# Two weight DMAs on two queues, 33 warm-up matmuls and two clamps on VectorE in a linear-attention and gated-MLP block

## The chip, the cores and the metric

The kernel runs on one core of a Trainium2 chip. A core has TensorE (PE, matmuls; its weight loads are listed as PEld), VectorE (DVE), ScalarE (ACT), GpSimd (POOL) and SyncE (SP), which here only issues DMAs. The engines run side by side, each through its own instructions in order, and wait for each other by semaphores. The metric is the device time of one execution in microseconds; lower is better.

## The reference

The input x has 2048 tokens of 448 features. The block is linear attention with 16 heads of 28 features, behind a LayerNorm, and a gated MLP with 1792 hidden features, behind another one; both add to their input. All tensors are bfloat16.

```python
def _A_ref(x, wqkv, wo):
    q, k, v = split(x @ wqkv)                       # 16 heads of 28
    phi = lambda t: jnp.where(t > 0, t + 1, jnp.exp(t)) + 1e-6
    pq, pk = phi(q), phi(k)
    kv = jnp.einsum("bhsd,bhse->bhde", pk, v)
    z = jnp.einsum("bhsd->bhd", pk)
    num = jnp.einsum("bhqd,bhde->bhqe", pq, kv)
    den = jnp.einsum("bhqd,bhd->bhq", pq, z)[..., None] + 1e-6
    return merge(num / den) @ wo

def _B_ref(x, w_gate, w_up, w_down):
    return (_gelu(x @ w_gate) * (x @ w_up)) @ w_down

h = x + _A_ref(_layernorm(x), A_wqkv, A_wo)
h2 = h + _B_ref(_layernorm(h), B_w_gate, B_w_up, B_w_down)
```

## The kernel before, in words

Tokens are worked in 16 tiles of 128. Every piece of work is a named task on one engine, and the tasks' order on each engine is written out in full in `ORDERS` (line 14), one string for each of PE, ACT, DVE, POOL and SP. A task that needs another engine's result waits for that engine's counter; a DMA has a semaphore of its own. An engine does not look past a task that waits. A number behind a name is the tile (k14 is the K and V matmuls of tile 14) or, for gu, the group.

1. *Start.* PE runs `warm1` and `warm0` (line 457: `WARM` matmuls of 128 columns on ones), which need no input. Meanwhile the x tiles are loaded. For each tile `bnst`, `bnag` (VectorE) make mean and variance, `ln`, `rstd` (ScalarE) the factor, and `norm` the normalised tile: on VectorE for tiles 0 to 3, on GpSimd for the others, with the negated mean from `negm`.
2. *Transposes.* Tiles 0 to 3 are transposed on PE (`tr`, line 495) and copied out of PSUM by ScalarE (`ev`). Tiles 4 to 15 get 64 of their columns copied by ScalarE (`dup`) and are transposed by a DMA on SyncE (`xT`).
3. *K and V, queries.* `k` and `v` of a tile (lines 561 and 562) are 14 matmuls that use the two row halves of PE at once, on two PSUM banks that they fill crosswise. ScalarE makes the exponential (`ek`) and copies V (`evv`), `cl` clamps the exponential (line 566), `ph` on VectorE adds max(K, eps) to the clamped value, and `acc..a`, `acc..b` add K-transposed times V into banks 6 and 7. The two `acc` halves of a tile use the banks crosswise, and so wait for each other when they are neighbours of different kind. Query chunks (`qa`, `qb`) stand between, with `eq` (ScalarE), `cq` (clamp, GpSimd) and `pq` (sum, VectorE); for later chunks `rq` on ScalarE and `cq`, `pq` on VectorE.
4. *Hand-over.* `kz1`, `kz2` mask the sums, `nd` multiplies with the queries, `rd` and `om` divide, `tro`/`evo` or the DMA `oT` transpose, `wo` is the output projection, `hr` the residual add, and the second LayerNorm follows with `hbnst`, `hbnag`, `hln`, `hrstd`, `normh`. `wrap` copies a few columns so that the transposed halves are complete; for tiles 0 and 1 PE transposes (`trh`, line 702) and `evh` copies out.
5. *MLP.* The 56 groups `gu` (line 811) make gate and up on the two row halves, `ge` is the Gelu on ScalarE (after the table load `tbl2`), `hm` the product on VectorE, `down` the last projection, `out` the residual and `dout` the store. The remaining `nd`, `wo` and LayerNorm work is spread between the groups.

The gate and up weights lie in one tile, `wgu_sb`: gate in partitions 0 to 63, up in 64 to 127, seven slices of 64 rows each. They come by fourteen DMAs, gate and up by turns, all on SyncE, after the last `xT` and the four loads of `wo`:

```python
for k in range(7):
    prev = [dma(wgu_sb[0:64, k, :], wg3[:, k, :], [b_wg[k]], "dwg%d" % k, 64 * FF * 2, after=prev, key=20.0)]
    prev = [dma(wgu_sb[64:128, k, :], wu3[:, k, :], [b_wu[k]], "dwu%d" % k, 64 * FF * 2, after=prev, key=20.0)]
```

The down weights (`dwd`) follow behind oT2 and oT3.

## Time and profile before

| | |
|---|---|
| median of 3 runs | 196.68 us (196.2 to 196.69) |
| the profiled execution | 196.7 us, of which its span is 194.9 |
| PE busy | 190.3 us, 98% of the span |
| DVE, ACT, POOL busy | 116.3, 78.2, 42.0 us |
| PE matmuls of gate and up | 980, 90.4 us busy |
| PE matmuls of down (row halves / whole array) | 336, 34.4 us / 70, 10.8 us |
| DMA | 17.53 MB, 90 GB/s over the span |

In the rows below, a timeline line is the start, the length of the stretch, engine, source line, operation, output and inputs, and the count of instructions merged; square brackets give the engine's idle time before it and what ended it. A line of a group gives busy time, the mean of one in ns, and the idle time before. A row of stages gives the stretch, its length, the busy us of PE, PEld, DVE, ACT and POOL with their instructions, the granted clock, the share of DMA time and GB/s. Line 430 is the helper of nearly all paired matmuls, so these are told apart by their tiles.

### The profile page before, as it was taken

The numbers are of one execution on the slowest core, as the hardware profiler recorded it, in microseconds if no ns is written. First come the engines' busy times: TensorE is split into PE (matmuls) and PEld (weight loads), VectorE is DVE, ScalarE is ACT, GpSimd is POOL, SyncE is SP. The second block draws the span as 40 slices with busy tenths as digits, with TensorE's granted clock in tenths as the row PEclk, the third lists the DMA queues.
The fourth block names the chain that finished last, engine by engine and source line by source line (L and its number), as shares of the span: only waits on it lengthen the run. The fifth ranks groups of instructions, "written<-read, shape, count | busy, mean of one in ns | idle before, by whom it ended". The sixth has DMA issues, their size and how long they took to land.

```text
span 194.9 us, 5336 instructions
## 1 busy us (share of the span) xinstructions
PE 190.3 (98%) x2192; PEld 137.9 (71%) x2192; DVE 116.3 (60%) x301; ACT 78.2 (40%) x205; POOL 42.0 (22%) x90
## 2 busy tenths in 40 slices
PE   7999999999999999999999999999999999999994
PEld 7556658754588977976675577877778779899554
DVE  2989735368998946843967745756735443431512
ACT  3689866669784212220442441233232442411100
POOL 3099974300050310500500500500500000000000
PEclk9999999999999999999999999999999999999999
DMA  6944558999836052152062250172040000010111
GB/s 191 377 116 97 81 110 185 247 248 205 260 103 110 15 101 50 50 105 62 10 129 46 46 106 2 30 117 51 5 94 28 23 0 0 3 47 3 47 47 47
DMA packets 37256, 17.53 MB, mean 90 GB/s; under 512 B 28272, under 2 KB 36336, under 8 KB 37232
## 3 DMA queue, kind: packets, MB, share of 16 engines
q1 hardware_dynamic: 36352, 16.45, 36.8%
q10 hardware_dynamic: 880, 0.75, 1.2%
q8 instruction: 17, 0.28, 0.6%
q14 instruction: 7, 0.06, 0.1%
HBM read 8.72 MB, written 1.84 MB: 54 GB/s over the span
## 4 chain that ended last, share of the span: by engine, by line
PE 96%; issue 1%; ACT 1%; DVE 1%; POOL 0%; DVEq 0%; ACTq 0%; POOLq 0%
PE ps L430 87%; PE ps L780 6%; PE ps L454 2%; DVE x_sb L660 1%; PE ps L495 1%; ACT xn L617 1%; PE ps L681 0%; ACT xnT L523 0%; PE ps L672 0%; DVE x_sb L756 0%; POOL ones_bf L395 0%; POOL eps_t L398 0%; ACT pqT L616 0%; DVEq L196 0%; ACTq L196 0%
## 5 line engine op out<-in xcount | busy, mean ns | idle before, releaser
L430 PE MATMUL ps<-hnT,wgu_sb 64*128 64x512 bf16 (+1 forms) x980 | 90.4, 333 | 0.0
L430 PEld LDWEIGHTS ps<-hnT,wgu_sb 64*128 64x128 bf16 x980 | 64.5, 94 | 18.6 <-DVE hh L832 1.7
L830 ACT ACTIVATE gl<-ps 128x256 bf16<-128x256 f32 x112 | 36.9, 381 | 89.3 <-PE ps L430 88.2
L832 DVE TENSOR_TENSOR hh<-ps,gl 128x256 bf16<-128x256 f32 x112 | 42.5, 415 | 35.7 <-ACT gl L830 31.5
L430 PE MATMUL ps<-wd_sb,hh 64*128 64x448 bf16 x336 | 34.4, 349 | 0.0
L430 PEld LDWEIGHTS ps<-wd_sb,hh 64*128 64x128 bf16 x336 | 25.6, 94 | 6.2 <-DVE x_sb L756 0.2
L430 PE MATMUL ps<-wkv_sb,xnT 64*128 64x448 bf16 x192 | 22.4, 350 | 0.4 <-ACT xnT L523 0.4
L462 DVE BATCH_NORM_STATS2 st<-x_sb 128x6 f32<-128x448 bf16 x32 | 18.7, 611 | 2.6 <-DMA x_sb<-in_A_x_dram 2.6
L756 DVE TENSOR_TENSOR x_sb<-ps,x_sb 128x448 bf16<-128x448 f32 (+1 forms) x17 | 9.9, 591 | 16.6 <-PE ps L430 9.8
L474 POOL TENSOR_SCALAR ln<-mv 128x2 f32<-128x2 f32 x7 | 1.6, 223 | 75.0 <-DVE mv L463 74.9
L568 DVE SCALAR_TENSOR_TENSOR pk<-ps,tm 128x448 bf16<-128x448 f32 x16 | 9.8, 620 | 9.6 <-POOL tm L566 7.1
L430 PE MATMUL ps<-xnT,wq_sb 64*128 64x512 bf16 x112 | 14.9, 377 | 0.2 <-ACT xn L617 0.2
L430 PEld LDWEIGHTS ps<-wkv_sb,xnT 64*128 64x128 bf16 x192 | 10.1, 94 | 6.3 <-issue 0.8
L430 PE MATMUL ps<-wo_sb,oT 64*128 64x448 bf16 x98 | 12.1, 350 | 0.1
L660 DVE TENSOR_TENSOR x_sb<-ps,x_sb 128x448 bf16<-128x448 f32 x16 | 9.4, 618 | 4.6 <-PE ps L430 4.4
L780 PE MATMUL ps<-wd_sb,hh 128*128 128x448 bf16 (+1 forms) x70 | 10.8, 315 | 0.0
L566 POOL TENSOR_SCALAR tm<-e 128x448 bf16<-128x448 bf16 x16 | 8.9, 559 | 6.4 <-ACT e L565 5.5
L487 POOL TENSOR_SCALAR hn<-x_sb,nm,rs 128x448 bf16<-128x448 bf16 x14 | 10.0, 720 | 0.8 <-POOL rs L476 0.2
L565 ACT ACTIVATE e<-ps 128x448 bf16<-128x448 f32 x16 | 8.5, 541 | 3.5 <-PE ps L430 2.2
L780 PEld LDWEIGHTS ps<-wd_sb,hh 128*128 128x128 bf16 x70 | 6.7, 98 | 4.3 <-issue 0.4
L655 DVE TENSOR_TENSOR o_sb<-ps,rd 128x448 bf16<-128x448 f32 x16 | 9.4, 612 | 0.1
L570 ACT ACTIVATE v<-ps 128x448 bf16<-128x448 f32 x16 | 8.4, 542 | 2.1 <-PE ps L430 2.1
(69 smaller groups left out, 140.4 us busy)
## 6 DMA issues: line engine op xcount, KB each, us to landing
out_dram<-x_sb SPq DMA_DIRECT2D x15, 112.0 KB, 1.7
wgu_sb<-in_B_w_gate_dram SPq DMA_DIRECT2D x7, 224.0 KB, 6.1
wgu_sb<-in_B_w_up_dram SPq DMA_DIRECT2D x7, 224.0 KB, 6.4
wd_sb<-in_B_w_down_dram SPq DMA_DIRECT2D x1, 1568.0 KB, 8.3
x_sb<-in_A_x_dram SPq DMA_DIRECT2D x2, 448.0 KB, 5.3
wkv_sb<-in_A_wqkv_dram ACTq DMA_DIRECT2D x2, 336.0 KB, 3.7
x_sb<-in_A_x_dram SPq DMA_DIRECT2D x3, 224.0 KB, 4.2
wo_sb<-in_A_wo_dram SPq DMA_DIRECT2D x2, 336.0 KB, 4.4
```

The costliest lines, as they stand in the source:

```text
L430: ins = e.matmul(o_, l_, r_, start=s_, stop=p_, **kw)
L462: op("dve", lambda e: e.bn_stats(st[:, t, :], src_ap), [b_src], [b_st[t]], "%sbnst%d" % ("" if mv is mv1 else "h", t), 0.53, key, after=after)
L487: return lambda e: e.tensor_scalar(dst, src[:, t, :], nm[:, t:t + 1], rs[:, t:t + 1], ALU.add, ALU.mult)
L565: act_exp(lambda e: e.activation(e1[:, ie, :], oK, AF.Exp), bank(bk), [b_e1[ie]], "ek%d" % t, _c_act(D), kk)
L566: op("pool", lambda e: e.tensor_scalar(tm1[:, ie, :], e1[:, ie, :], 1.0 + EPS, 0.0, ALU.min, ALU.max), [b_e1[ie]], [b_tm1[ie]], "cl%d" % t ...
L568: op("dve", lambda e: e.scalar_tensor_tensor(pk[:, i, :, 0:GW], psK3, EPS, tm1[:, ie, :].rearrange("p (g e) -> p g e", g=NG), ALU.max, ALU ...
L655: op("dve", lambda e: e.tensor_tensor(o_sb[:, so, oc:oc + D].rearrange("p (a e) -> p a e", e=28), nd3[:, :, 0:28], rd[:, i, :].unsqueeze(2 ...
L660: op("dve", lambda e: e.tensor_tensor(h_sb[:, u, :], ps[:, b, 0:D], x_sb[:, u, :], ALU.add), bank(b) + [b_x[u]], [b_h[u]], "hr%d" % u, 0.5 ...
L756: op("dve", lambda e: e.tensor_tensor(x_sb[:, t, c0:c1], ps[:, bk, c0:c1], h_sb[:, t, c0:c1], ALU.add), bank(bk) + [b_h[t]], [bo], "out%d% ...
L780: ins = e.matmul(ps[:, bk, c0:c1], hh[:, j, hsl(t)], wd_sb[:, j, c0:c1], start=(j == 0), stop=(j == NJ - 1))
L830: G.add("act", lambda e, gi=gi, cs_=cs_, psG=psG: e.activation(gl[:, gi, cs_], psG[:, cs_], AF.Gelu_apprx_tanh), r=bank(BK_G[i]), w=[b_glh ...
L832: op("dve", lambda e, dst=dst, srcU=srcU, srcL=srcL: e.tensor_tensor(dst, srcU, srcL, ALU.mult), bank(BK_U[i]) + [b_glh], [b_ar[j_][t % HR ...
```

## The change

- The fourteen weight DMAs become two: `dwg`, all of gate, on SyncE behind the `wo` loads, and `dwu`, all of up, on ScalarE's queue. `dwu` waits for the last transposed x tile; it stands between ek13 and ek14 in ScalarE's order.
- `WARM` goes from 38 to 33.
- `cl14` and `cl15` run on VectorE, between ph13 and ph15, instead of GpSimd.
- `trh` waits for the wrapped columns only ahead of its seventh transpose.
- All five orders are written anew. What moves around the steps above: acc3a and acc4a go ahead of and behind q01's second half, acc8b and acc9b behind k11 and k12, acc13a and acc14a ahead of qa20, and acc15a behind qb20; qb31 goes from between wo2a and wo2b to behind trh0; ScalarE runs dup7 and dup6 ahead of ek3, evh0 ahead of eq14, and rq14 later; VectorE runs pkones first, om4 ahead of om5, and cq14 and cq10 behind hm1; GpSimd runs negm12 ahead of cq1, norm13 ahead of norm10, and powwarm at the start. Some gate/up groups near the end change places with the down groups between them.

```diff
-    "... v5 k6 qa01 v6 qb01 k7 acc3a acc4a v7 ..."
+    "... v5 acc3a k6 qa01 v6 qb01 acc4a k7 acc4b acc5b v7 ..."
-    "... k15 acc10a v14 acc10b acc11b v15 acc11a acc12a acc12b acc13b qa20 acc13a acc14a qb20 acc14b acc15b acc15a qa11 ..."
+    "... k14 k15 v14 acc10b acc11b v15 acc11a acc12a acc12b acc13b acc13a acc14a qa20 acc14b acc15b qb20 acc15a qa11 ..."
-    "... qa31 wo2a qb31 wo2b trh1 trh0 nd4a nd4b gu1 gu0 ..."
+    "... qa31 wo2a wo2b trh1 trh0 qb31 nd4a nd4b gu1 gu0 ..."
...
+    CL_DVE = cfg.get("cl_dve", (14, 15))
-    WARM = 38
+    WARM = 33
...
-        for k in range(7):
-            prev = [dma(wgu_sb[0:64, k, :], wg3[:, k, :], [b_wg[k]], "dwg%d" % k, 64 * FF * 2, after=prev, key=20.0)]
-            prev = [dma(wgu_sb[64:128, k, :], wu3[:, k, :], [b_wu[k]], "dwu%d" % k, 64 * FF * 2, after=prev, key=20.0)]
+        prev = [dma(wgu_sb[0:64, :, :], wg3, [*b_wg], "dwg", 7 * 64 * FF * 2, after=prev, key=20.0)]
+        dma(wgu_sb[64:128, :, :], wu3, [*b_wu], "dwu", 7 * 64 * FF * 2, q="act", r=[b_xnT[T - 1]], key=20.0)
...
-            op("pool", lambda e: e.tensor_scalar(tm1[:, ie, :], e1[:, ie, :], 1.0 + EPS, 0.0, ALU.min, ALU.max),
-               [b_e1[ie]], [b_tm1[ie]], "cl%d" % t, 0.53, kk)
+            op("dve" if t in CL_DVE else "pool", lambda e: e.tensor_scalar(tm1[:, ie, :], e1[:, ie, :], 1.0 + EPS, 0.0, ALU.min, ALU.max),
+               [b_e1[ie]], [b_tm1[ie]], "cl%d" % t, _c_dve(D, 4.0) if t in CL_DVE else 0.53, kk)
...
-            def ftrh(e):
+            def ftrh(e, W):
...
-                for k in (0, 1, 2, 4, 5, 6, 3):
+                for n, k in enumerate((0, 1, 2, 4, 5, 6, 3)):
+                    if n in (0, 6):
+                        W(n)
```

## The prediction

> **What bounds the kernel now.** I read the page first, then the busy time by stage, then the chain of work that ended last in order of time, then the timelines of single engines around each edited place.

> ```profile
> span 194.9 us, 5336 instructions
> PE 190.3 (98%) x2192; PEld 137.9 (71%) x2192; DVE 116.3 (60%) x301; ACT 78.2 (40%) x205; POOL 42.0 (22%) x90
> ```

> TensorE (PE) is busy in 190.3 of 194.9 us. The stages, in the view of busy time by stretch (each engine's busy us, its instructions in brackets), tell where it is not:

> ```profile
> 0.00:7.43 7.43, 6.02 (x75) 5.33 (x76) 3.79 (x13) 3.02 (x7) 1.62 (x13) 1.00 0.79 254
> 7.43:41.44 34.01, 33.82 (x437) 21.18 (x437) 22.52 (x53) 25.82 (x71) 22.59 (x42) 1.00 0.71 164
> 41.44:54.13 12.69, 12.23 (x133) 6.30 (x134) 10.85 (x28) 10.39 (x16) 0.00 (x0) 1.00 0.99 241
> 54.13:181.72 127.59, 127.47 (x1489) 98.42 (x1482) 75.18 (x203) 38.31 (x112) 17.84 (x35) 1.00 0.24 50
> ```

> From 54.13 to 181.72, the gate/up/down stage, PE idles 0.12 us in 127.59. The change adds and removes no matmul there, so nothing is to be won in that stage; it can only begin earlier. So the whole question is when the first gate/up group (gu1) starts, 54.13 now. Before it lie the warm-up and first transposes (to 7.43), the K/V stage and the hand-over to the second LayerNorm. The chain agrees:

> ```profile
> 2.00 4.17 PE ps L454 x38
> 6.17 0.50 PE ps L495 x9
> 6.68 0.60 ACT xnT L523
> ...
> 7.43 0.95 PE ps L430 x8
> ...
> 52.26 1.17 DVE x_sb L660 x2
> ...
> 103.35 78.37 PE ps L430 x776
> ```

> The 38 warm-up matmuls are on the chain, then the transposes tr0, its evacuation ev0 on ScalarE and the first K matmuls k0. Much later 1.17 us of two residual adds (hr2, hr3) on VectorE stand between the attention output and gu1.

> **1. Five warm-up matmuls fewer.**

> ```profile
> 1.93 4.24 PE L454 MATMUL ps<-ones_bf 128*128 128x128 bf16 x38
> 5.21 0.37 DVE L486 TENSOR_SCALAR xn<-x_sb,mv,rs 128x448 bf16<-128x448 bf16 x1
> 5.97 0.40 DVE L486 TENSOR_SCALAR xn<-x_sb,mv,rs 128x448 bf16<-128x448 bf16 x1
> 6.09 0.86 PEld L495 LDWEIGHTS ps<-ident,xn 64*128 64x128 bf16 x20 [0.20 <-DVE pk L399]
> ```

> From the first warm-up matmul to the first weight load of tr0 are 6.09 - 1.93 = 4.16 us for 38, 0.11 each; five give 0.55 us, and tr0 could go at 5.54. But its input is norm0, which ends at 5.21 + 0.37 = 5.58; with 0.1 to 0.15 us for the semaphore it goes at about 5.72. So 0.37 us of the 0.55 arrive. The second transpose needs norm1, which ends at 6.37 either way (moving the memset pkones away leaves norm1 behind its own rstd1), so tr1 now follows tr0 with a gap, at about 6.45; ev0 needs only tr0, and with it k0 moves by the full 0.37, to 7.06. Kept: 0.37 us, bounds 0 and 0.37. It is 0 if what k0's successors wait for doesn't move too; that is the second rival.

> **2. Clamp of K tiles 14 and 15 on VectorE, and the order around it.**

> ```profile
> 37.27 0.56 POOL L566 TENSOR_SCALAR tm<-e 128x448 bf16<-128x448 bf16 x1 [1.78 <-ACT e L565]
> 37.96 0.62 DVE L568 SCALAR_TENSOR_TENSOR pk<-ps,tm 128x448 bf16<-128x448 f32 x1 [1.71 <-POOL tm L566]
> 38.11 0.54 PEld L430 LDWEIGHTS ps<-xnT,wq_sb 64*128 64x128 bf16 x7 [0.25 <-ACT v L570]
> 40.30 0.11 PEld L430 LDWEIGHTS ps<-v,pk 64*128 64x128 bf16 x4 [0.23 <-PE ps L430]
> L618 DVE TENSOR_SCALAR pqT<-pqT 112x1024 bf16<-112x1024 bf16 x5 | 2.0, 407 | 0.0
> L749 DVE COPY hn<-hn 128x448 bf16<-128x448 bf16 x14 | 3.5, 273 | 1.0 <-POOL hn L487 0.9
> ```

> cl14 takes 0.56 us on GpSimd, and ph14 on VectorE begins 0.13 after it. VectorE is idle for 1.71 us just there. The trace has no such clamp on VectorE; by its own two-operation clamp of 1024 columns (407 ns) and its copy of 448 columns (273 ns) it costs 0.25 to 0.3, nearer the copy of equal width. So ph14 and ph15 each come about 0.56 + 0.13 - 0.27 = 0.4 us sooner. What PE makes of it is less: the new order runs acc13a and acc14a ahead of qa20 and acc14b, acc15b ahead of qb20. That removes the pause of 0.23 at 40.30 (acc15b and acc15a use the two row halves of the same banks crosswise, and stand side by side now), but puts acc13b and acc13a side by side, which is a pause of the same kind. The wait of 0.25 at 38.11 is for evv15, which ScalarE now runs after ek15: it stays. The pauses around the accumulations are 0.23 + 0.25 in all, so the gain lies between -0.1 and 0.45; I take 0.15, a third, because one pause of the two kinds is exchanged for its like.

> **3. The hand-over.** Now qb31 stands between wo2a and wo2b; afterwards wo2a and wo2b are neighbours, the transposes trh1 and trh0 follow (their first six wait only for the norm, the seventh for the wrapped columns), then qb31, then nd4a.

> ```profile
> 53.04 0.22 PE L430 MATMUL ps<-kvz,pqT 64*128 64x116 bf16 x1
> 53.47 0.82 PE L430 MATMUL ps<-kvz,pqT 49*128 49x116 bf16 x15 [0.21 <-DVE x_sb L660]
> ...
> 62.84 0.30 PEld L430 LDWEIGHTS ps<-wo_sb,oT 64*128 64x128 bf16 x6 [0.50 <-PE ps L430]
> ```

> nd4a's first matmul goes at 53.04 and the rest at 53.47, when hr3 has freed its bank: 0.43 us. With qb31 in between that wait is covered. Against it stands the pause of neighbours that cross their banks, as wo4a and wo4b show at 62.84: 0.50 us at the loader, some 0.3 of it beyond a plain step. The difference is 0.13; the upper bound is the 0.43, the lower -0.1 (VectorE's string from hr1 to evh1 is not shorter, and gu1 needs evh1). I take 0.13. ScalarE runs evh0 ahead of eq14 now, which only helps gu1; eq14 and the table load then stand ahead of the first Gelu, below.

> **4. The weights.** Fourteen DMAs on SyncE become one there (dwg) and one on ScalarE (dwu), which waits for the last x transpose.

> ```profile
> L430 PEld LDWEIGHTS ps<-hnT,wgu_sb x980: 92/94/96, 54.1 to 181.1; 64*128 64x128 bf16 x196
> L364 SPq DMA_DIRECT2D wgu_sb<-in_B_w_up_dram x7: 596/596/1418, 32.4 to 40.9; - x7
> DMA to landing us min/median/max: 4.9/6.2/7.7
> 0.80 1.00 ACTq L364 DMA_DIRECT2D wkv_sb<-in_A_wqkv_dram  x2
> 36.64 0.54 ACT L565 ACTIVATE e<-ps 128x448 bf16<-128x448 f32 x1 [0.94 <-PE ps L430]
> ```

> The last piece is issued at 40.9 and lands 4.9 to 7.7 later, by 48.6; the first use is at 54.1. That cover of 5.5 us hides any moderate change of the transfer, so it counts 0 on either side; SyncE's own time, twelve issues less, frees nothing that PE waits for, since the next transposes oT2 and oT3 wait for VectorE. The new cost is on ScalarE: dwu stands ahead of ek14, with evv14, ek15 and evv15 behind it, which acc14a and qa20 wait for. An issue there took 0.50 (1.00 for two), on SyncE 0.596 with one of 1.418. ScalarE is idle for 0.94 ahead of ek14 (36.64). So 0 at 0.5 to 0.6, which I take, being ScalarE's own row; 0.5 if it is 1.42.

> **Sum**, against the profiled execution's own 196.7 us (span 194.9 and 1.8 around it; the median of the runs shown is 196.68): 196.7 - 0.37 - 0.15 - 0.13 = 196.05; I say 196.0. About 0.3%, 0.59 us, is what a measurement of this kernel can tell from no change, so this is just outside.

> **Rivals.** *The clock (slower).* Warm-up is there for the matmul clock:

> ```profile
> L454 PE MATMUL ps<-ones_bf 128*128 128x128 bf16 x11 | 1.4, 314 | 0.0
> L495 PE MATMUL ps<-ident,xn 64*128 64x64 bf16 x12 | 0.7, 235 | 0.0
> L702 PE MATMUL ps<-ident,hn 128*128 128x128 bf16 x14 | 1.0, 220 | 0.0
> ```

> To the last warm-up matmul (window 5 to 6.05) one takes 314 ns and in tr0 and tr1 (6.05 to 7.2) a transpose 235, while 128 columns take 220 in the transposes at 52 us: PE is still slow after 38 warm-ups (the granted clock reads 1.00 in the first stage too, so the durations are the evidence), and k0 at 7.43 finds it fast only just (8 matmuls in 0.95 us). With 5 fewer the opening may come after k0 has begun. If it takes another stretch as long as the warm-up (4.24 us) at half speed, 2.1 us are lost: 196.0 + 2.1 = 198.1; if only the missing 0.55 us must be made up, 0.3: 196.3. It decides when the speed has not risen by the time of k0. For it: the margin here is a few tenths. Against: the gap ahead of k0 shrinks, and tr0 and tr1 keep PE occupied. Chance 0.15. [...]

> *The shift is eaten on the way (within 0.3%).*

> ```profile
> 16.75 1.19 POOL L626 TENSOR_SCALAR tm<-e 112x512 bf16<-112x512 bf16 x2
> 18.74 0.30 PEld L430 LDWEIGHTS ps<-wkv_sb,xnT 64*128 64x128 bf16 x6 [0.29 <-DVE pqT L627]
> 56.35 0.75 DVE L832 TENSOR_TENSOR hh<-ps,gl 128x256 bf16<-128x256 f32 x2
> ```

> k6 at 18.74 waits for the first queries' sums on VectorE, which wait for two clamps on GpSimd at 16.75. GpSimd is full there, and its new order puts a small operation (negm12) ahead of them; ScalarE's new order runs two copies (dup7, dup6) ahead of ek3, which the clamps also follow. If GpSimd's string doesn't move, k6 stays at 18.74 and only 0.1 of the 0.37 is left (acc3a now runs before k6). Likewise the third gate/up group needs hm1, at 56.35 to 57.10 on VectorE, behind om4 and om5 in the new order, with eq14 and the table load ahead of its Gelu. Then the sum is 0.1 + 0.15 + 0 = 0.25, and the time 196.45; 196.1 to 197.2 with the bounds. Chance 0.34.

> *ScalarE held by dwu (slower).* If its issue takes 1.42 or more, as one on SyncE did, and it meets a late x transpose, 0.6 to 1.0 us pass on to acc14a and qa20: 197.3 to 197.7, deciding from 0.94 us on. Chance 0.09.

> **Numbers.** The forecast has 0.42, its own range 195.6 to 196.1 (upper bounds of steps 2 and 3). Faster 0.42; within 0.3% 0.34; slower 0.15 + 0.09 = 0.24. The range 195.6 to 197.5 takes in the first two cases and half of the last, 0.80, and leaves out the clock.

> **What would show it.** tr0 at about 5.7 and k0 at 7.06 with 8 matmuls still in 0.95 us (step 1; a k0 of 1.5 us or more is the clock); k6's wait for VectorE below 0.3 and its start near 18.4 (else it was eaten); ph14 0.4 us after ek14's end, and acc15a done before 40.1 (step 2); nd4a in one piece and gu1 at 53.5 (step 3); the last weight landed before 50 and dwu's issue at 0.6 (step 4). Wrong it is if gu1 isn't earlier than 53.6, or if the stretch from gu1 to the end is longer than now.

## The result, and the profile after

The changed kernel takes 198.49 us (median of 6 executions, 197.81 to 200.63), the kernel before on the same chip 196.48 (6 executions, 196.16 to 196.69). The ratio is 1.0115, with a 95% interval of 1.0066 to 1.0164: slower, where 196.0 was forecast, and outside the range up to 197.5. The profiled execution took 198.26, its span is 196.5 where it was 194.9. The ratios here and below are of executions in the faster of two states, which leaves out only three of the twelve of one experiment (e1).

From the page of the changed kernel:

```profile
span 196.5 us, 5313 instructions
PE 190.4 (97%) x2187; PEld 127.9 (65%) x2187; DVE 117.2 (60%) x303; ACT 77.9 (40%) x205; POOL 41.8 (21%) x88
```

PE is busy as long as before, and the span is 1.6 us longer: PE waits. Busy time in the stretches used for the kernel before:

```profile
0.00:7.43 7.43, 6.00 (x75) 5.07 (x77) 3.82 (x13) 3.44 (x7) 2.04 (x14) 1.00 0.79 257
7.43:41.44 34.01, 33.78 (x443) 21.10 (x440) 23.25 (x57) 25.46 (x71) 21.14 (x39) 1.00 0.66 148
41.44:54.13 12.69, 11.05 (x106) 4.86 (x104) 9.25 (x25) 8.39 (x14) 0.00 (x0) 1.00 1.12 275
54.13:181.72 127.59, 127.28 (x1491) 89.58 (x1489) 76.31 (x205) 39.91 (x114) 18.60 (x35) 1.00 0.26 50
```

Up to 41.44 PE does 443 matmuls where it did 437: it is ahead. From 41.44 to 54.13 it is busy for 11.05 us where it was 12.23. The loss begins in the hand-over. PE's own timeline there:

```profile
48.50 1.04 PE L431 MATMUL ps<-xnT,wq_sb 64*128 64x512 bf16 x8 [0.19 <-ACT xn L618]
50.74 0.35 PE L431 MATMUL ps<-wo_sb,oT 64*128 64x448 bf16 x1 [1.21 <-DVE hn L487]
51.27 1.72 PE L431 MATMUL ps<-wo_sb,oT 64*128 64x448 bf16 x13 [0.18 <-DVE hn L696]
55.12 1.58 PE L431 MATMUL ps<-hnT,wgu_sb 64*128 64x256 bf16 x26
```

qa31 starts at 48.50, wo2a should follow 0.86 us later (it did before: 49.21 to 50.07), at 49.36, and starts at 50.74. The page names a VectorE instruction as what ended the wait, but wo2a doesn't read `hn`. It reads `oT`, which a DMA transpose fills. When that lands is told by the tile's DMAs and by the DMAs issued from 44 to 51 us. The kernel before:

```profile
DMA to landing us min/median/max: 2.4/2.5/4.2
oT<-o_sb SPq DMA_TRANSPOSE x2, 3.1
```

The changed kernel:

```profile
DMA to landing us min/median/max: 2.4/2.5/5.9
oT<-o_sb SPq DMA_TRANSPOSE x2, 5.5
wgu_sb<-in_B_w_gate_dram SPq DMA_DIRECT2D x1, 1568.0 KB, 16.6
wgu_sb<-in_B_w_up_dram ACTq DMA_DIRECT2D x1, 1568.0 KB, 16.2
```

The median of the 14 transposes of `oT` is 2.5 us from issue to landing, in both kernels. oT2, the first one, took 3.46 us before and takes 5.89 now: it is issued 0.7 us sooner (44.77 instead of 45.48) and lands 1.7 later (50.65 instead of 48.94). (The 4.2 in the first view is not oT2 but the first transpose behind the down weights, issued at 56.29, when the gate and up weights had long landed; the second one there took 4.2 in the changed kernel too. What holds those isn't known.) dwg and dwu, issued at 33.31 and 33.87, land at 49.88 and 50.11, the last weight of the kernel before at 48.45.

Starts of some tasks, in us (the last residual is VectorE's last operation ahead of the last store):

| task | before | after | difference |
|---|---|---|---|
| tr0 / k0 | 6.10 / 7.43 | 5.61 / 6.89 | -0.49 / -0.54 |
| k6 | 18.74 | 18.39 | -0.35 |
| acc15a | 40.30 | 39.65 | -0.65 |
| qa31 | 49.21 | 48.50 | -0.71 |
| wo2a | 50.07 | 50.74 | +0.67 |
| gu1 | 54.13 | 55.12 | +0.99 |
| wo4a | 61.77 | 63.14 | +1.37 |
| last residual | 192.56 | 194.11 | +1.55 |

So 0.71 us were won by qa31, 1.38 lost ahead of wo2a, 0.32 between wo2a and gu1, 0.38 from gu1 to wo4a and 0.18 later: +1.55.

### The profile page after: what moved, and what is told of

Its sections match the earlier page's. It is cut to its first block, busy times and chain, and to the rows that moved or that the text cites. A ratio compares the mean times of both kernels' runs of the same rounds, so it can differ in the third digit from the quotient of the medians.

```text
span 196.5 us, 5313 instructions
## 1 busy us (share of the span) xinstructions
PE 190.4 (97%) x2187; PEld 127.9 (65%) x2187; DVE 117.2 (60%) x303; ACT 77.9 (40%) x205; POOL 41.8 (21%) x88
## 3 DMA queue, kind: packets, MB, share of 16 engines
q1 hardware_dynamic: 35696, 14.84, 34.1%
## 4 chain that ended last, share of the span: by engine, by line
PE 89%; DVE 4%; ACT 2%; DMA 2%; issue 1%; SPq 0%; DVEq 0%
PE ps L431 82%; PE ps L783 5%; DMA x_sb<-in_A_x_dram 2%; DVE hh L835 1%; DVE st L463 1%; ACT L853 1%; DVE x_sb L661 1%; PE ps L496 1%; ACT hnT L710 0%; ACT pqT L617 0%; PE ps L705 0%; DVE pqT L620 0%; PE ps L689 0%; PE ps L682 0%; ACT ln L468 0%
## 5 line engine op out<-in xcount | busy, mean ns | idle before, releaser
L431 PE MATMUL ps<-hnT,wgu_sb 64*128 64x512 bf16 (+1 forms) x980 | 91.8, 333 | 0.1
L431 PEld LDWEIGHTS ps<-hnT,wgu_sb 64*128 64x128 bf16 x980 | 61.7, 94 | 23.0 <-DVE hh L835 5.1
L431 PE MATMUL ps<-wd_sb,hh 64*128 64x448 bf16 x336 | 35.2, 349 | 0.0
L431 PEld LDWEIGHTS ps<-wd_sb,hh 64*128 64x128 bf16 x336 | 21.2, 94 | 11.1 <-DVE x_sb L759 0.2
L431 PE MATMUL ps<-wo_sb,oT 64*128 64x448 bf16 x98 | 13.0, 350 | 1.6 <-DVE hn L487 1.2
L482 POOL TENSOR_SCALAR nm<-mv 128x2 f32<-128x2 f32 x13 | 2.9, 226 | 39.5 <-DVE mv L464 39.1
L488 POOL TENSOR_SCALAR hn<-x_sb,nm,rs 128x448 bf16<-128x448 bf16 x14 | 10.6, 764 | 0.8 <-POOL rs L477 0.2
L566 ACT ACTIVATE e<-ps 128x448 bf16<-128x448 f32 x16 | 8.7, 541 | 3.8 <-PE ps L431 3.4
L431 PEld LDWEIGHTS ps<-wo_sb,oT 64*128 64x128 bf16 x98 | 6.3, 94 | 5.7 <-DVE hn L487 1.7
## 6 DMA issues: line engine op xcount, KB each, us to landing
wgu_sb<-in_B_w_gate_dram SPq DMA_DIRECT2D x1, 1568.0 KB, 16.6
```

What stands on the lines that cost most here:

```text
L431: ins = e.matmul(o_, l_, r_, start=s_, stop=p_, **kw)
L482: op("pool", lambda e: e.tensor_scalar(nm[:, a:b], mv[:, a:b, 0], -1.0, None, ALU.mult), b_mv[a:b], b_nm[a:b], "%snegm%d" % ("" if mv is m ...
L488: return lambda e: e.tensor_scalar(dst, src[:, t, :], nm[:, t:t + 1], rs[:, t:t + 1], ALU.add, ALU.mult)
L566: act_exp(lambda e: e.activation(e1[:, ie, :], oK, AF.Exp), bank(bk), [b_e1[ie]], "ek%d" % t, _c_act(D), kk)
```

## The experiments

Each batch ran on one chip together with the kernel before, which took 196.41 to 196.60 us there. The theory that held is called the landing: oT2 completes about 0.5 us after the last of the weights issued ahead of it, on whichever queue (0.42 to 0.59 us in the 14 profiles in which weights were still in flight), so the start and the length of the weights' stream set wo2a.

### One part of the change undone or done alone

**e1**, the changed kernel with the fourteen transfers: dwg and dwu replaced by the old loop, all on SyncE.

> The changed kernel with the fourteen weight DMAs by turns on SyncE as before; all else as changed. Three theories of the pause ahead of wo2a (PE idle from 49.4 to 50.7, waiting for the transposes oT2 and oT3). Form: one long DMA ahead of oT2 in SyncE's queue has a late straggler; then with fourteen pieces oT2 lands below 49.0, the pause goes and the time is about 196.2. Late start: what delays oT2 is that the last x transpose is issued 1.8 us later than before (29.2 against 27.4) and the whole weight stream behind it; then the last weight lands near 50.4 here too, oT2 behind it, and the time stays at 198.0 or more. Order: qb31 behind trh0 and the other moves cost it by themselves; then oT2 is early and the time is still above 197.

197.88 us (median of nine executions, 196.50 to 198.25; three more took 199.96 to 201.36), ratio 1.0057 (1.0039 to 1.0075). In the profile (197.98) the pause is still there. PE's timeline:

```profile
50.51 0.35 PE L433 MATMUL ps<-wo_sb,oT 64*128 64x448 bf16 x1 [0.96 <-DVE hn L489]
```

The first transfer leaves at 33.39, as dwg did (33.31), and the last weight lands at 49.94 (50.11). With the same start the form is worth 0.2 us at the landing in these two executions. Over all of them it may be worth more: the ratio is below the changed kernel's 1.0115, though the intervals overlap, and three of the nine took 196.50 to 197.13. None of those three has a profile, so the form's share is open.

**e2**, the kernel before with only the two transfers, dwu behind ek13.

> The kernel before with the two weight DMAs alone: dwg on SyncE, dwu on ScalarE behind ek13. Form: dwg lands 16.6 us after its issue near 31.9, so at 48.5, or later by a straggler; oT2 lands at 49 to 50.5 against a need at 50.07, so between no change (196.5) and 0.8 us more (197.3). Late start: the stream starts as early as before, so no change, 196.5. The prediction's step 4 said 0.

198.32 us (197.75 to 200.56), ratio 1.0119 (1.0077 to 1.0161). So the part that was counted at 0 costs 1.9 us alone, 1.6 in the median of the four executions whose clock did not fall. dwg leaves at 31.65, but dwu only at 33.88, and lands at 50.69; oT2 lands at 51.24. PE's timeline, and two stretches of busy time (the number ahead of the last two is the granted clock):

```profile
51.33 0.35 PE L431 MATMUL ps<-wo_sb,oT 64*128 64x448 bf16 x1 [1.52 <-DVE pqT L618]
```

```profile
52.49:55.91 3.42, 3.42 (x23) 1.45 (x20) 0.54 (x1) 1.02 (x1) 0.00 (x0) 0.50 0.92 318
55.91:60.00 4.09, 3.92 (x72) 3.17 (x72) 3.72 (x12) 2.94 (x5) 1.02 (x3) 1.00 0.00 0
```

Shortly behind the pause of 1.52 us the clock stood at half for 3.42 us in this execution, which took 200.09 and has a mean clock of 0.991. The other at 0.991 took 200.56, the four at 0.999 or 1.0 took 197.75 to 198.49. The changed kernel's execution of 200.63 has 0.991 too.

**e3**, the changed kernel with dwg on ScalarE's queue too, right ahead of dwu, so that nothing of the weights stands ahead of oT2 on SyncE's queue.

> The changed kernel with both weight DMAs on ScalarE's queue at dwu's place, dwg ahead of dwu, so that oT2 and oT3 stand behind no weights in SyncE's queue while just as many bytes are in flight beside them. Form and late start both put the delay on the queue ahead of oT2: then oT2 lands within 4 us of its issue at 44.8, the pause ahead of wo2a goes, and the time falls by about 1.4 to 2, to 196.2 to 196.8 (the second issue on ScalarE may cost up to 0.3). If it is the sharing of the DMA engines and not the queue, oT2 still lands after 50 and the time stays near 198.

204.15 us (202.93 to 205.30), ratio 1.0395 (1.0363 to 1.0426). DMAs issued, and PE's timeline:

```profile
wgu_sb<-in_B_w_gate_dram ACTq DMA_DIRECT2D x1, 1568.0 KB, 12.7
wgu_sb<-in_B_w_up_dram ACTq DMA_DIRECT2D x1, 1568.0 KB, 18.5
oT<-o_sb SPq DMA_TRANSPOSE x2, 8.4
```

```profile
53.68 3.52 PE L432 MATMUL ps<-wo_sb,oT 64*128 64x448 bf16 x14 [4.10 <-issue]
```

The weights come one after the other, the last at 53.07, and oT2 at 53.59, on a queue of its own. A theory that a transpose waits for what stands ahead of it on its queue falls here. oT2 had been issued at 44.81; the DMA engines' packets from 45 to 50 us:

```profile
DMA packets 287, 1.03 MB, mean 205 GB/s; under 512 B 1, under 2 KB 1, under 8 KB 287
q10 hardware_dynamic: 287, 1.03, 103.9%
```

All of them are of ScalarE's queue (q10). SyncE's queue moved nothing for 5 us, though oT2 stood on it.

**e4**, the kernel before with `WARM = 33`.

> The kernel before with 33 warm-up matmuls instead of 38 and nothing else. Step 1 of the prediction: k0 0.4 to 0.5 us earlier; what follows k0 moves with it as far as gu1 if no queue stands in the way: 196.0. If oT2 and oT3, which stand behind the weights and landed at 48.9 and 49.4 against a need at 50.07, are the next bound, they still leave 0.7 us, so the gain is kept. Clock rival: a granted clock clearly below 0.999 in some runs, and those 1.5 to 2 us longer.

196.36 us (12 executions), ratio 1.0012 (0.9991 to 1.0034): no difference. But nine lie at 196.17 to 196.60 and three at 197.87 to 198.01. The profiled execution (197.96) is one of the three; its PE timeline at k0, and below it that of f3 (further down), which has 38:

```profile
7.34 1.30 PE L430 MATMUL ps<-wkv_sb,xnT 64*128 64x448 bf16 x6
```

```profile
7.26 0.74 PE L432 MATMUL ps<-wkv_sb,xnT 64*128 64x448 bf16 x6 [0.36 <-ACT xnT L525]
```

k0's first six matmuls take 1.30 us there and 0.74 in f3, and the first record of full speed (350 ns for one, up to 578 before) is at 10.47 us. The granted clock reads 1.00 all the while, against the expectation; the durations are the evidence. This is the first rival in a quarter of the executions, 1.7 us above the others where it was priced at 2.1.

### When the weights start

**e5**, the changed kernel with the weights earlier: `wo`'s loads among the x transposes, dwg right behind xT15, dwu ahead of ek11 and without its wait for the last transposed tile.

```diff
-xT9 xT10 xT11 xT12 xT13 xT14 xT15 dwo dwo_t dwo_u dwo_s dwg
+xT9 dwo dwo_t xT10 xT11 dwo_u dwo_s xT12 xT13 xT14 xT15 dwg
-eq5 ek11 ek12 evv11 evv12 evv13 ek13 dwu ek14
+eq5 dwu ek11 ek12 evv11 evv12 evv13 ek13 ek14
```

> The changed kernel with nothing altered but when the weights start: the four wo transfers are issued among the x transposes (two behind xT9, two behind xT11), dwg right behind xT15 and dwu on ScalarE ahead of ek11, both without a wait. Theory of the landing (oT2 completes about 0.5 us after the last weight, wherever that is issued; the two weight DMAs need 16.3 us from issue): issue near 30.8, last weight near 47.3, oT2 at its own 2.4 to 3 us (47.3 to 48), wo2a right behind qa31 near 49.4 with a pause under 0.2, gu1 53.4 to 53.7, time 195.8 to 196.5. Theory of the form (two transfers side by side hurt by themselves, e.g. what PE reads and writes): still 197.5 or more. Theory of the order (qb31 behind the transposes costs): pause gone but gu1 near 54.1 to 54.3, time 196.6 to 197.2.

205.12 us (204.49 to 205.66), ratio 1.0441 (1.0421 to 1.0460): every expectation missed, and for the theory's own reason. dwu left at 29.41 and landed at 39.84; the x transposes of tiles 14 and 15, issued at 28.79 and 31.28 on the other queue, landed at 40.21 and 40.82, 0.37 and 0.98 behind it. PE's timeline and busy time:

```profile
40.35 1.30 PE L432 MATMUL ps<-wkv_sb,xnT 64*128 64x448 bf16 x6 [5.31 <-DMA xnT<-xn]
```

```profile
37.05:43.88 6.83, 3.53 (x20) 1.75 (x22) 0.40 (x1) 0.00 (x0) 0.00 (x0) 0.50 1.12 208
```

Here the releaser is named: the transposes. The clock fell to half within the pause, at 37.05, for 6.83 us.

**f1**, the kernel before, with its fourteen transfers and its order, and one knob: the first weight transfer waits for evv12.

```diff
+        b_gate = _Buf("gate")
...
+            r = [b_gate]
...
+                prev = [dma(wgu_sb[0:64, k, :], wg3[:, k, :], [b_wg[k]], "dwg%d" % k, 64 * FF * 2, r=r, after=prev, key=20.0)]
...
+                r = []
...
+               bank(bv), [b_v1[i]] + ([b_gate] if t == 12 else []), "evv%d" % t, _c_act(D), kk - 0.5)
```

> The kernel before, with fourteen weight transfers and its own order, and one knob: the first weight transfer waits for evv12 on ScalarE (ends near 34.1), where it left at 31.9. Theory of the landing: everything of the weights moves by 2.3 us, the last weight to near 50.7, oT2 to 51.2, wo2a from 50.1 to 51.3, gu1 from 54.1 to 55.3, time 197.4 to 197.9. If it is the two transfers, the order of the tasks or the warm-up that costs, this kernel is as before, 196.3 to 196.7, since gu1 needs the weights only at 54.1, over 3 us after they have landed.

197.51 us (197.12 to 197.96), ratio 1.0049 (1.0034 to 1.0065), within the expected 197.4 to 197.9, though the landings came sooner than expected. The start is 2.0 us later (33.83), the last weight 1.3 (49.78, expected 50.7), oT2 lands at 50.26 (expected 51.2), oT3 at 50.74. DMAs issued from 44 to 51 us and PE's timeline:

```profile
oT<-o_sb SPq DMA_TRANSPOSE x2, 4.7
```

```profile
50.35 0.35 PE L430 MATMUL ps<-wo_sb,oT 64*128 64x448 bf16 x1 [0.38 <-DVE st L462]
50.87 0.91 PE L430 MATMUL ps<-wo_sb,oT 64*128 64x448 bf16 x7 [0.17 <-DVE hn L486]
```

wo2a is late by 0.56 and gu1, at 54.91, by 1.06 against qa31's 48.93. gu1 needs the weights 5 us after they have landed, and still the later start costs 0.9 us. That a later stream delays oT2, wo2a and gu1 is shown by this: two transfers, new orders and warm-up are all absent here.

### What makes them start later

In the changed kernel xT12 leaves at 25.31 (before 23.47) and xT15 at 29.21 (27.37); `wo` and the weights stand right behind. ScalarE's timeline names a cause, dup12 waiting for norm12 on GpSimd, which the new order puts behind cl6, cq3, cq2 and cl7; dup12 itself now stands behind ek7 and evv7. Neither move is in the list of the change above.

```profile
25.03 0.26 ACT L526 ACTIVATE xn<-xn 128x64 bf16<-128x64 bf16 x1 [0.94 <-POOL xn L488]
```

**e7** moves norm12 from behind cl7 to behind norm11; **e9** also moves dup12 ahead of ek7 and dup14 ahead of ek9.

> The changed kernel with one GpSimd task moved: norm12 right behind norm11 instead of behind cl7. Theory of the landing, with GpSimd's new order as what made the weights late: xT12 leaves near 23 where it left at 25.3, xT15 near 27.5 to 28, dwg near 31.6 to 32, last weight 48.2 to 48.6, oT2 48.8 to 49.1, wo2a 49.0 to 49.3, gu1 53.6 to 54.0, time 196.0 to 196.9. If GpSimd's order is not what holds the x transposes, nothing moves: 198.0 to 198.5. Price to set against a gain: the clamps cl6 to cl8 come up to 0.7 us later and may hold the accumulations.

> The changed kernel with three small tasks back where they let the x transposes go earlier: norm12 right behind norm11 on GpSimd, dup12 ahead of ek7 and dup14 ahead of ek9 on ScalarE (moving norm12 alone left xT12 behind dup12). Theory of the landing, with the new order around norm12 as what made the weights late: xT12 leaves near 23.3 where it left at 25.3, xT15 near 27.5 to 28, dwg near 31.6, last weight 48.2 to 48.8, oT2 0.5 us behind it, wo2a at 49.0 to 49.5, gu1 53.4 to 53.9, time 196.0 to 196.9. If the start of the weights isn't what counts, 198.0 to 198.8 as the changed kernel.

e7: 198.62 us (198.44 to 200.28), ratio 1.013 (1.0101 to 1.0160). e9: 200.24 (198.99 to 201.96), ratio 1.0199 (1.0163 to 1.0235). Neither gave the gain. Four of e7's six executions took 198.44 to 198.66, close to what its expectation has for the case that GpSimd's order isn't what holds the x transposes; five of e9's six have a granted clock of 0.991. The profiles can't tell why: both fell on executions in which full speed came late (k4 at 16.79 and 16.74 where it was 14.98), so that ScalarE and the transposes were late anyway (xT15 at 31.21 and 29.92). In e9 dwu left 1.7 us behind dwg and the last weight landed at 52.43, oT2 at 52.99. That norm12 or dup12 delays the weights is read from the trace and not shown by a run, and e7 speaks against norm12 as the only cause.

**e6** moves qb31 ahead of wo2a, into the wait. **e8** sets `WARM = 38` in the changed kernel.

> The changed kernel with one TensorE task moved: qb31 (0.82 us by the timeline) ahead of wo2a instead of behind trh0. Theory of the landing: wo2a does not move (50.6 to 50.8, the landing of oT2 sets it), qb31 is done inside the wait, nd4a follows trh0 at once and may pay the 0.43 us for its bank again: gu1 54.3 to 54.9 where it was 55.1, time 197.6 to 198.3. Theory of the order (the placing of qb31 is what was lost): gu1 back near 53.6, time 196.2 to 196.6.

> The changed kernel with 38 warm-up matmuls. Theory of the landing: the weights' issue hangs on GpSimd and SyncE, not on TensorE, so tr0 and k0 come 0.5 us later (k0 near 7.4) but wo2a stays at 50.6 to 50.9 and gu1 at 55.0 to 55.2: 198.0 to 198.6, no difference; what the five warm-ups gave is lost in the wait. Theory of the clock (33 warm-ups leave the speed of TensorE uncertain later on): faster than the changed kernel by 0.5 or more. Theory of a shift that is passed on: slower by 0.5, 198.9 to 199.1.

e6: 200.08 us (199.47 to 200.62), ratio 1.0181 (1.0161 to 1.0200), slower than either theory said. From wo2a to gu1 it takes 4.36 us, as with qb31 behind (4.38): hr2 and hr3 on VectorE follow wo2b and end at 55.27, evh1 at 55.79, gu1 starts at 56.01; PE had nothing to gain. wo2a itself stood at 51.65, since the weights landed at 51.00, 0.9 us later than in the changed kernel; 0.5 of that is a later start (33.80), the rest isn't known. e8: 198.76 us (198.30 to 201.23), ratio 1.014 (1.0100 to 1.0179), no different from the changed kernel. But the profile doesn't bear out the expectation of the landing, that k0 alone moves: k0 comes 0.33 us later, the weights leave at 34.12 and land at 50.62, and wo2a (51.24) and gu1 (55.62) are 0.50 later too. So it isn't shown that the wait swallows what the warm-up gains.

### The first three steps with the landing out of the way

**e10**, the changed kernel with the weights in two column parts: 0 to 1023 where dwg and dwu stand, 1024 to 1791 behind oT2 and oT3, `wd` behind oT5. **e11** is e10 with qb31 between wo2a and wo2b, **e12** is e10 with `WARM = 38`.

```diff
+FL = 1024
-        prev = [dma(wgu_sb[0:64, :, :], wg3, [*b_wg], "dwg", ...
+        prev = [dma(wgu_sb[0:64, :, 0:FL], wg3[:, :, 0:FL], [*b_wg], "dwg", ...       (up likewise, on ScalarE)
+        dma(wgu_sb[0:64, :, FL:FF], wg3[:, :, FL:FF], [b_wgh], "dwgh", ...            (up likewise, on SyncE)
-oT2 oT3 dwd oT4 oT5
+oT2 oT3 dwgh dwuh oT4 oT5 dwd
```

> The changed kernel with the weights' columns in two parts: 0 to 1023 of both halves where dwg and dwu stand now, 1024 to 1791 in two more transfers on SyncE's queue behind oT2 and oT3 (first read by gu5, about 6 us after gu1), and wd behind oT5. Theory of the landing: the first part needs 16.5 * 1024/1792 = 9.4 us from 33.3, ends near 43 to 44.5 ahead of oT2's issue at 44.8; oT2 lands 2.4 to 3 us after its issue (47.2 to 47.8), wo2a goes right behind qa31 at 49.3 to 49.5, gu1 at 53.6 to 53.8, and the gain of 0.7 us that the changed kernel has at qa31 arrives: 195.7 to 196.3. Rivals: the second part holds oT4 and oT5 in the same way, wo4a then waits, 196.5 to 198; or the form itself is what hurts, 198 or more.

> The kernel with the two column parts, and qb31 back between wo2a and wo2b: the hand-over of before on the undisturbed base. The prediction's third step says the new order is worth 0.13 us (-0.1 to 0.43). From the changed kernel's profile the opposite: there gu1 follows wo2a by 4.38 us where it was 4.06 before, since wo2b still ends ahead of hr2, hr3 and evh1 on VectorE, which gu1 waits for. So by that reading this kernel is the same or faster than the one with qb31 last, by 0 to 0.4 us; by the prediction's step it is slower by 0.1 to 0.4.

> The kernel with the two column parts, and 38 warm-up matmuls. The prediction's first step says that the five fewer are worth 0.37 us at k0; with no landing in the way the shift should be passed on, so this kernel is slower by 0.3 to 0.5 than the one with 33. Rival, the clock: with 33 some executions open the clock only near 10 us (seen in two profiles, at a price of 1.5 us there), with 38 fewer do; then the medians are equal and the slowest runs are those with 33. Rival, a shift that is eaten: the same within 0.1.

PE's timeline in e10:

```profile
49.52 1.74 PE L432 MATMUL ps<-wo_sb,oT 64*128 64x448 bf16 x14
53.39 3.84 PE L432 MATMUL ps<-hnT,wgu_sb 64*128 64x256 bf16 x65
68.18 1.05 PE L432 MATMUL ps<-hnT,wgu_sb 64*128 64x256 bf16 x16 [3.21 <-DMA hnT<-hn]
```

oT2 lands 2.48 us after its issue, wo2a waits for nothing, and gu1 starts at 53.39, 0.74 ahead of the kernel before. Then gu7 waits 3.21 us for transposes of the second LayerNorm's output, issued behind `wd` (67.38 and 68.09, `wd` at 66.41). So the times say nothing of the steps (three of e10's six executions, one of e11's and three of e12's have a granted clock of 0.991): 200.56 us (1.0202, 1.0160 to 1.0244), 200.05 (1.0191, 1.0156 to 1.0226) and 200.23 (1.0196, 1.0158 to 1.0234). The starts do. From wo2a to gu1 it is 3.87 us with the new order and 4.09 in e11: step 3 is worth 0.22 between these two executions, and my reading that it costs falls. k0 is at 7.05 with 33 and at 7.43 with 38, gu1 at 53.39 and 53.80: step 1 is worth 0.4 between these two executions.

**f2** takes 1280 columns in the first part and leaves `wd` at its place behind the second; **f3** is f2 with `WARM = 38`; **f4** gives the kernel before the same parts.

> The changed kernel with the weights' columns in two parts, 0 to 1279 where dwg and dwu stand now and 1280 to 1791 in two transfers behind oT2 and oT3, wd right behind them as before. Theory of the landing: the first part (71%) ends near 45 to 47, oT2 lands at 47.4 to 47.8, wo2a at 49.4 without a pause, gu1 at 53.4; the second part and wd end near 58.5, oT4 and oT5 land by 59.5, ahead of wo4a at 61.3. What the prediction's first three steps are worth then reaches the end: 0.4 to 0.75 us below the kernel before, 195.7 to 196.1. Rival: the transposes behind it (oT4, oT5, hT3, hT2) are held again, wo4a or gu7 waits, 196.5 to 199.

> The same column parts with 38 warm-up matmuls. Against the one with 33: slower by 0.3 to 0.45 if the prediction's first step (0.37 us) reaches the end; equal if the shift is eaten or if 33 lose in late openings of the clock what they gain.

> The kernel before, with the first 1280 columns in its fourteen transfers and the other 512 in two behind oT2 and oT3. In the kernel before wo2a has 0.7 us in hand after oT3's landing, so nothing waits there and nothing is to be gained: 196.2 to 196.7. If the kernel before loses something to the landing too, it gets faster, by 0.3 or more. If the second part holds oT5 and oT4, slower.

f2: 197.33 us (197.06 to 198.87), ratio 1.0054 (1.0033 to 1.0075). f3: 197.55 (197.34 to 197.65), 1.0050 (1.0038 to 1.0062). f4: 197.28 (196.82 to 197.67), 1.0040 (1.0026 to 1.0053). f2's PE timeline:

```profile
61.47 0.35 PE L432 MATMUL ps<-wo_sb,oT 64*128 64x448 bf16 x1
62.08 1.73 PE L432 MATMUL ps<-wo_sb,oT 64*128 64x448 bf16 x13 [0.25 <-DMA oT<-o_sb]
```

gu1 is at 53.46, 0.67 ahead, but the second part and `wd` now end at 59.63, oT4 and oT5 land at 60.16 and 62.03, and wo4a waits: the rival named in the expectation. f4 pays the same, so the column parts cost by themselves.

**g1** is the kernel before with the first three steps and nothing of the weights, its queues and the rest of its orders as they were; **g2** is g1 with `WARM = 38`.

> The kernel before with the first three steps of the change and nothing of the weights: 33 warm-up matmuls, the clamps of tiles 14 and 15 on VectorE with the new order of the accumulations, and the new hand-over (wo2a, wo2b, the transposes, qb31). The queues of SyncE and ScalarE and the rest of GpSimd's list stay as before. By the prediction's sum 0.37 + 0.15 + 0.13 = 0.65 us less: 195.8 to 196.0. Theory of the landing adds a floor: oT3 lands at 49.4 in the kernel before and wo2a starts at 50.1, so up to 0.7 us can be won before wo2a waits for it; 195.8 to 196.2. Rival: the gain is eaten behind gu1 (gu5 and wo4a came 0.3 us late in the changed kernel even where nothing waited for a transpose): 196.2 to 196.6. Executions in which the clock opens late would stand 1.5 us higher.

> The same with 38 warm-up matmuls, so without the first step. By the prediction's sum 0.28 us less than the kernel before, 196.1 to 196.3, and 0.37 more than with 33. If the warm-up gains nothing over whole runs (the kernel before with 33 alone was 196.36 beside 196.46), it equals the kernel with 33 within 0.15.

g1: 197.73 us (197.61 to 199.35), ratio 1.0094 (1.0062 to 1.0125). g2: 197.80 (197.63 to 197.99), 1.0067 (1.0054 to 1.0079). Both missed. PE's and ScalarE's timelines in g1:

```profile
55.02 1.16 PE L433 MATMUL ps<-hnT,wgu_sb 64*128 64x256 bf16 x18 [1.32 <-DVE pqT L622]
```

```profile
53.09 1.02 ACT L620 ACTIVATE pqT<-ps 112x1024 bf16<-112x1024 f32 x1 [2.15 <-PE ps L433]
54.01 0.91 ACT L713 ACTIVATE hnT<-ps 128x896 bf16<-128x896 bf16 x1
```

wo2a starts at 49.67 with nothing to wait for, 0.4 ahead of before. But I had left ScalarE's order as it was, eq14 ahead of evh0. eq14 waits for qb31, which now stands behind the transposes, and evh0 waits for eq14: gu1 waits 1.32 us. The new hand-over needs evh0 ahead of eq14, as the changed kernel has it. No version here beat the kernel before.

## Why the prediction was wrong

**Step 4 failed**, at two sentences. "That cover of 5.5 us hides any moderate change of the transfer" measures the cover to gu1, the reader of the weights. The one that suffers shares no data with them: oT2, in flight at the same time. And "SyncE's own time, twelve issues less, frees nothing that PE waits for, since the next transposes oT2 and oT3 wait for VectorE" holds for their issue and was taken for their landing. The profile before had the warning, oT2's own 3.46 us to landing beside a median of 2.5. In 14 profiles with weights still in flight oT2 landed 0.42 to 0.59 us after the last of them, for last landings from 48.1 to 53.1; in the other six (e5, e10, e11, e12, f3, f4), where they were in at the latest 1.9 us after its issue, it took 2.42 to 2.48. Term by term: counted 0, measured by e2 alone 1.9 us. In the changed kernel's profile it is the later start, 1.44 us (33.31 instead of 31.87), which no term of the prediction has, and 0.2 for the form, with e1's caveat.

**Step 1**, forecast tr0 5.72, k0 7.06, 0.37 us at most: 5.61, 6.89, 0.54 in this execution. Over others it is 0.38 (e12 against e10), 0.14 (f3, f2) and nothing (g2, 6.98; g1, 6.99), with the first record of full speed anywhere from 4.1 us (f1) to 7.4 (e12): in f3 the 38 matmuls took 4.18 us, the 20 transposes behind them 0.85, and k0 came at 7.26; in the kernel before it was 4.24, 0.96 and 7.43. Whole executions show no gain (e4). The clock rival exists: of 26 executions with 33 in e4, f2 and g1, six stand over a microsecond above the others of their kernel, none of 24 with 38 in f1, f3, f4 and g2, and none of 70 of the kernel before, all at or below 196.91. The late opening itself is in e4's profile (and in those of e7 and e9, with 33 too); for the other five it is inferred.

**Step 2** was right in its signs: ph14 starts 0.41 us after ek14's end (forecast 0.4), acc15a starts at 39.65 (forecast: done before 40.1). That the lead grows by 0.17 from k0 to qa31, where 0.15 was forecast, is in part luck: it falls from 0.54 at k0 to 0.35 at k6, as the second rival said, and rises to 0.65 at acc15a. And the wait for evv15 ahead of qa20, 0.25 us, that was to stay is gone.

**Step 3** was right where nothing else waits: nd4a in one piece, gu1 at 53.39 and 53.46 (forecast 53.5), 0.22 from the order. The prediction named evh0's move as help; by g1 it is a condition worth 1.3 us.

**The second rival** also came true behind gu1, though with another pair than the one named (the third group and hm1): gu5, the fifth, waits for hm3, and hm3 for pq10. VectorE's timeline of the changed kernel, and of the one before:

```profile
59.76 1.04 DVE L620 TENSOR_TENSOR pqT<-xn,pqT 112x1024 bf16<-112x1024 bf16 x1
60.91 0.74 DVE L835 TENSOR_TENSOR hh<-ps,gl 128x256 bf16<-128x256 f32 x2
```

```profile
58.92 0.68 DVE L619 TENSOR_TENSOR pqT<-xn,pqT 112x1024 bf16<-112x1024 bf16 x1
59.52 0.75 DVE L832 TENSOR_TENSOR hh<-ps,gl 128x256 bf16<-128x256 f32 x2
```

hm3 starts 5.79 us behind gu1 where it started 5.39, and from gu5 to wo4a it takes 1.82 us where it took 1.53 (1.53 in f1 too, 1.82 in e10). **The third rival** did not: dwu's issue took 0.65 us. Two sums are off, without weight here: its 197.3 to 197.7 adds the loss to 196.7 and not to the forecast, and the upper bounds of steps 2 and 3 give 195.45, not 195.6.

Without the landing the changed kernel's rows would sum to -0.71 at qa31, -0.19 to gu1 (3.87 instead of 4.06) and +0.56 behind it: -0.34, an estimate, where -0.65 was forecast. No run shows it over a whole execution.

## What to carry to other kernels

Ahead of moving or merging a large load, list every DMA that is issued while it is in flight, transposes above all, and ask when each lands, not when it is issued; the cover of the load's own reader, 5.7 us here (48.45 to 54.13), said nothing of them. Where a DMA's time to landing is well above its median, as oT2's 3.46 us beside 2.5, ask what is in flight beside it, even where nothing waits for it yet. Where a reordering puts one task later, look on the other engines for what stands behind the task that waits for it.

## What the runs showed of the hardware

At first the two queues did not work side by side. The changed kernel's DMAs from 37 to 39 us, packets and share by queue (q1 is SyncE's, q10 ScalarE's):

```profile
DMA packets 118, 0.42 MB, mean 211 GB/s; under 512 B 0, under 2 KB 0, under 8 KB 118
q1 hardware_dynamic: 111, 0.40, 99.2%
q10 hardware_dynamic: 7, 0.03, 4.8%
```

from 42 to 44, and from 51 to 54, when `wd` comes into all 128 partitions:

```profile
DMA packets 207, 0.72 MB, mean 361 GB/s; under 512 B 9, under 2 KB 9, under 8 KB 206
DMA packets 1276, 1.14 MB, mean 381 GB/s; under 512 B 0, under 2 KB 1276, under 8 KB 1276
```

and the kernel before from 38 to 44, with its turns of gate and up:

```profile
DMA packets 518, 1.50 MB, mean 249 GB/s; under 512 B 104, under 2 KB 104, under 8 KB 517
```

Into 64 partitions, with seven packets for the others, the DMA engines moved 211 GB/s from 37 to 39 us, while SyncE's queue filled 99.2% of their time; with both halves at once, from 42 to 44, it was 361, and 249 with the turns of the kernel before. dwu had been issued over 3 us before 37, at 33.87, and got 7 of the 118 packets. In e3 from 45 to 50 SyncE's queue got none of 287, though oT2 had been issued on it at 44.81. Why is open.
